# Attention of the second and third token tile eight heads at a time, first loads in a fixed order, and two other matmul orders in layer 2

## The chip, the core and the metric

The kernel runs on one core of one Trainium2 chip. The time is device microseconds of one execution. A core has five instruction streams that run beside each other and wait for one another by semaphores: TensorE (PE, matmuls; its weight loads are shown as PEld), VectorE (DVE), ScalarE (ACT), GpSimd (POOL) and SyncE (SP, which here issues every DMA). Each stream is executed in the order in which it is written.

## What is computed

A local and global attention over 2 batches, 8 heads, 768 positions and 64 columns a head, followed by two feed-forward layers over the 1536 tokens. Cut to what matters:

```python
# attention: a window of +-15 positions, and 24 block summaries (blocks of 32)
k_sum = k.reshape(B, H, nb, block, D).max(axis=3)
v_sum = v.reshape(B, H, nb, block, D).mean(axis=3)
scores_l = scale * q @ k^T, -1e9 outside |i - j| < 16
scores_s = scale * q @ k_sum^T + log(32)
a = softmax(concatenate([scores_l, scores_s]))
attn = a @ concatenate([v, v_sum])
# two layers, 512 -> 2048 -> 512 each
h = x @ w_in;  g = h * sigmoid(1.702 * h);  x = g @ w_out      # layer 1
h = x @ w_in;  g = h * cos(h);              x = g @ w_out      # layer 2
```

All is float32. The feed-forward products are made of three matmuls each, on a high and a low part of both operands (high x high, low x high, high x low).

## The kernel before

**Tiles.** Tokens go in three tiles of 512 (`U`). A layer works through the 16 slices of 128 of `d_ff`, tile after tile: 48 steps a layer, 96 in all. A step has 12 matmuls of 512 columns for `h` (`ff_h`, lines 651 to 653: four slices `k` of the input by three products) and 12 for the output (`ff_out`, lines 744 to 746: four slices `d`, each into its own bank `acc0` to `acc3`). So there are 2304 of these matmuls, here called the FF matmuls. Between `h` and `out` stands the gate (`ff_gate`, ScalarE and VectorE). The weights come packed from memory, one `raw` tile of 1024 KB for two slices (`w_load`), and `convert` takes them apart into high and low part on ScalarE and VectorE: `w scale`, `w low`, `w join`, two `w hi`, two `w lo`. In layer 1 this runs about a step ahead of its use.

**Attention.** A unit (`att`) is 128 queries of four heads: scores `s` (TensorE, line 425), mask and maximum `ttr` (VectorE, line 434, one instruction a head), `exp` (ScalarE, line 443), the sum and its reciprocal (lines 450, 452) and `norm` (line 456) on VectorE, the transposes `t` (TensorE, line 461), their copy `at` (ScalarE, line 465), and the products with the values `pv` (TensorE, line 472). For the first token tile (`early`, eight units) `xc` (ScalarE, line 504) and `xl` (VectorE, line 507) then write the input `xh` of layer 1. The first `h` matmul of slices k = 0, 1 needs the four units of heads 0 to 3, that of k = 2, 3 the other four. The 16 units of the second and third tile (`main_unit`) are spread over the steps 0 to 30, between FF matmuls; their `xc` (line 519) writes `xf`.

**Loads.** All of `k` (`kf`) and 512 queries (`qf`) of the first batch are loaded for the early units. The values come as windows of 96 rows, four heads at a time (`load_v`, line 314), into `win` and `vy`; the main units have windows of `k` and `q` too (`load_k`, line 325, and `load_q`). The block means of `v` are made from `vf`: sums on POOL (line 371), a matmul `vs_ps` (line 382) and copies into the last 24 rows of each window (`put_vsum`, lines 349 and 353). Those of the second batch take seven sums on POOL and one matmul, `vsum1`.

**What sets the order.** Every step is an `Op` with a kind, an engine, a cost and what it depends on. `order_of` lists them by urgency, the length of the chain behind an `Op` plus a number for its kind from the table `BONUS`, and the program is written out in that order, for all engines and for the DMA issues of SP. The `Ring`s are the buffers: PSUM banks `a0`, `a1`, `acc0` to `acc3` and two `h`, the slots of the weights, `raw`, `win` and others.

## Time and profile before

| | |
|---|---|
| median of 3 runs | 607.96 us (607.31 to 608.61) |
| profiled execution, own time | 610.31 us |
| its span, first to last instruction | 608.5 us |
| TensorE busy in the span | 589.0 us |
| VectorE, ScalarE, GpSimd busy | 402.7, 298.4, 17.0 us |
| first FF matmul starts | 43.93 us |
| last FF matmul starts | 604.53 us |

A matmul's record is longer than the distance to the next one, because matmuls are pipelined; whether TensorE is held up is read from the distances of the starts. Records on VectorE and ScalarE overlap a little in the same way. A waiting time is put down to the engine whose semaphore came last.

### The profile page before, as it was taken

The numbers are of one execution on the slowest core, as the hardware profiler recorded it, in microseconds if no ns is written. First come the engines' busy times: TensorE is split into PE (matmuls) and PEld (weight loads), VectorE is DVE, ScalarE is ACT, GpSimd is POOL, SyncE is SP. The second block draws the span as 40 slices with busy tenths as digits, with TensorE's granted clock in tenths as the row PEclk, the third lists the DMA queues.
The fourth block names the chain that finished last, engine by engine and source line by source line (L and its number), as shares of the span: only waits on it lengthen the run. The fifth ranks groups of instructions, "written<-read, shape, count | busy, mean of one in ns | idle before, by whom it ended". The sixth has DMA issues, their size and how long they took to land.

```text
span 608.5 us, 8715 instructions
## 1 busy us (share of the span) xinstructions
PE 589.0 (97%) x3310; PEld 474.1 (78%) x3310; DVE 402.7 (66%) x826; ACT 298.4 (49%) x617; POOL 17.0 (3%) x20
## 2 busy tenths in 40 slices
PE   7759999999999999999999999999999999999997
PEld 4547777777777888888888888888888888888886
DVE  5688999965444432467778876667756668666664
ACT  4677788755544322356556643234433334433332
POOL 3240000000000000000000000000000000000000
PEclk8879999999999999999999999999999999999999
DMA  8998778552120500025553000000100000100001
GB/s 293 227 279 280 254 253 270 193 181 71 56 49 23 208 1 1 0 71 205 178 181 128 1 2 0 1 0 1 57 13 0 1 2 0 70 1 1 0 1 69
DMA packets 27817, 55.07 MB, mean 91 GB/s; under 512 B 10752, under 2 KB 19840, under 8 KB 23680
## 3 DMA queue, kind: packets, MB, share of 16 engines
q1 hardware_dynamic: 27776, 54.52, 27.3%
q8 instruction: 26, 0.43, 0.3%
q14 instruction: 15, 0.12, 0.1%
HBM read 51.37 MB, written 3.15 MB: 90 GB/s over the span
## 4 chain that ended last, share of the span: by engine, by line
PE 91%; DMA 4%; DVE 2%; ACT 1%; issue 1%; SPq 0%; ACTq 0%
PE h_ps L651 15%; PE acc L744 15%; PE h_ps L652 14%; PE h_ps L653 14%; PE acc L745 14%; PE acc L746 14%; PE x_ps L472 2%; PE t_ps L461 2%; PE s_ps L425 2%; DMA kf<-in_kT_dram 1%; DMA vf<-in_v_dram 1%; DMA raw<-in_w_dram 1%; DVE ex L434 0%; DVE ex L456 0%; DVE z L450 0%
## 5 line engine op out<-in xcount | busy, mean ns | idle before, releaser
L651 PE MATMUL h_ps<-xh,w 128*128 128x512 f32 x384 | 153.2, 399 | 0.0
L744 PE MATMUL acc<-g,w 128*128 128x512 f32 x384 | 151.4, 394 | 0.0
L652 PE MATMUL h_ps<-xh,w 128*128 128x512 f32 x384 | 150.1, 391 | 0.0
L653 PE MATMUL h_ps<-xh,w 128*128 128x512 f32 x384 | 150.1, 391 | 0.0
L745 PE MATMUL acc<-g,w 128*128 128x512 f32 x384 | 149.6, 390 | 0.0
L746 PE MATMUL acc<-g,w 128*128 128x512 f32 x384 | 149.6, 390 | 0.0
L705 ACT CAST g<-gt 128x512 fp32r<-128x512 f32 x96 | 59.7, 622 | 125.1 <-PE acc L746 121.7
L709 DVE TENSOR_TENSOR g<-gt,g 128x512 fp32r<-128x512 f32 x96 | 66.1, 689 | 65.9 <-ACT g L705 65.9
L744 PEld LDWEIGHTS acc<-g,w 128*128 128x128 f32 x384 | 72.1, 188 | 16.6 <-issue 1.7
L651 PEld LDWEIGHTS h_ps<-xh,w 128*128 128x128 f32 x384 | 72.3, 188 | 15.8 <-issue 0.6
L653 PEld LDWEIGHTS h_ps<-xh,w 128*128 128x128 f32 x384 | 72.4, 189 | 15.4
L746 PEld LDWEIGHTS acc<-g,w 128*128 128x128 f32 x384 | 72.1, 188 | 15.2
L745 PEld LDWEIGHTS acc<-g,w 128*128 128x128 f32 x384 | 72.1, 188 | 14.4
L652 PEld LDWEIGHTS h_ps<-xh,w 128*128 128x128 f32 x384 | 72.5, 189 | 14.0
L697 ACT ACTIVATE gt<-gt,half_pi 128x512 f32<-128x512 f32 x48 | 34.7, 723 | 62.1 <-DVE gt L693 62.1
L673 ACT ACTIVATE gt<-h_ps 128x512 f32<-128x512 f32 x48 | 28.7, 598 | 54.1 <-PE h_ps L653 53.8
L681 DVE TENSOR_SCALAR gt<-gt 128x512 f32<-128x512 f32 x48 | 20.5, 427 | 48.3 <-ACT gt L673 47.9
L701 DVE TENSOR_TENSOR gt<-gt,h_ps 128x512 f32<-128x512 f32 x48 | 33.0, 687 | 26.2 <-ACT gt L697 26.2
L603 DVE TENSOR_TENSOR w<-wc,w 128x512 fp32r<-128x512 f32 x64 | 42.9, 686 | 0.3 <-ACT w L599 0.3
L582 DVE SCALAR_TENSOR_TENSOR wc<-wc,raw 128x1024 uint32<-128x1024 uint32 x32 | 39.3, 1229 | 2.4 <-ACT wc L572 1.4
L572 ACT ACTIVATE wc<-raw 128x1024 f32<-128x1024 f32 x32 | 37.1, 1160 | 6.0 <-DMA raw<-in_w_dram 5.5
L599 ACT CAST w<-wc 128x512 fp32r<-128x512 f32 x64 | 38.4, 621 | 0.4 <-DVE wc L582 0.3
(66 smaller groups left out, 494.8 us busy)
## 6 DMA issues: line engine op xcount, KB each, us to landing
raw<-in_w_dram SPq DMA_DIRECT2D x32, 1024.0 KB, 5.0
win<-in_v_dram SPq DMA_DIRECT2D x40, 96.0 KB, 3.0
win<-in_kT_dram SPq DMA_DIRECT2D x32, 96.0 KB, 3.3
out_dram<-xf SPq DMA_DIRECT2D x12, 256.0 KB, 2.0
win<-in_qT_dram SPq DMA_DIRECT2D x16, 128.0 KB, 3.2
kf<-in_kT_dram SPq DMA_DIRECT2D x4, 400.0 KB, 6.1
k<-in_kT_dram SPq DMA_DIRECT2D x4, 400.0 KB, 5.6
vf<-in_v_dram SPq DMA_DIRECT2D x3, 512.0 KB, 7.4
```

What stands on the lines that cost most here:

```text
L572: nc.scalar.activation(out=t.bitcast(FP32), in_=raws[m][:, :, 1].bitcast(FP32), func=ACTF.Prelu, scale=REBIAS, alpha=SIGN)
L582: nc.vector.scalar_tensor_tensor(out=t, in0=t, scalar=3, in1=raws[m][:, :, 0], op0=ALU.logical_shift_left, op1=ALU.bitwise_or)
L599: nc.scalar.copy(out=w[:, 0, :], in_=mids[m][:, 512 * a:512 * (a + 1)].bitcast(FP32))
L603: nc.vector.tensor_tensor(out=w[:, 1, :], in0=mids[m][:, 512 * a:512 * (a + 1)].bitcast(FP32), in1=w[:, 0, :].bitcast(FP32), op=ALU.subtract,)
L651: nc.tensor.matmul(out=hs[i], lhsT=w[:, 0, c], rhs=x[:, 0, :], start=(k == 0), stop=False)
L652: nc.tensor.matmul(out=hs[i], lhsT=w[:, 1, c], rhs=x[:, 0, :], start=False, stop=False)
L653: nc.tensor.matmul(out=hs[i], lhsT=w[:, 0, c], rhs=x[:, 1, :], start=False, stop=(k == KD - 1))
L705: nc.scalar.copy(out=g[:, 0, :], in_=gts[i])
L709: nc.vector.tensor_tensor(out=g[:, 1, :], in0=gts[i], in1=g[:, 0, :].bitcast(FP32), op=ALU.subtract)
L744: nc.tensor.matmul(out=o, lhsT=w[:, 0, c], rhs=g[:, 0, :], start=(f == 0), stop=False)
L745: nc.tensor.matmul(out=o, lhsT=w[:, 1, c], rhs=g[:, 0, :], start=False, stop=False)
L746: nc.tensor.matmul(out=o, lhsT=w[:, 0, c], rhs=g[:, 1, :], start=False, stop=(f == NF - 1))
```

## The change

**Units.** The early part keeps its eight units of four heads (`early_unit`). The second and third tile get eight units of all eight heads (`main_unit`): 16 instead of 8 score matmuls in a row, eight `ttr` and eight `exp`, one sum and reciprocal, two `norm`, eight transposes, two `at`, 16 instead of 8 products, one `xc`. Numbers (`nm`, `z`, `r`) lie beside the scores and no longer in a pool of their own; the main units' buffers `sm_main` and `at_main` are slots of `w1`, those of the early units six and four deep instead of three.

**Loads.** Windows of `v` are laid out by the host (`vwin`) and come for all heads in one DMA with 4 KB a row. The list `wanted` makes each of the first loads wait for the issue of the one before it, and what comes later waits for the last of them.

**Layer 2.** In `ff_h` the products of low weights come first, so that the second and third matmul of a slice have the same weights. In `ff_out` two slices `d` go side by side: each product for `d` and `d + 1` in turn, into two banks.

**The table.** `BONUS` has other numbers, and some costs are other ones.

```diff
 BONUS = {
-    "at": 1927.8, "early at": -1746.5, "early exp": 2659.8, "early load w": -427.0, "early norm": -4559.3,
+    "at": 6913.9, "early at": 11300.1, "early exp": -9024.5, "early load v": -3298.6, "early load w": -5638.8,
...
-PUT_VSUM = ("ACT", "POOL")
+PUT_VSUM = ("ACT", "POOL", "POOL")
...
-    at_early = [ex[0][:, 512 * j:512 * j + 512] for j in range(3)]
-    sm_early = [ex[0][:, 1536:2016], ex[1][:, 0:480], ex[1][:, 480:960]]
+    sm_early = [ex[j // 4][:, 512 * (j % 4):512 * (j % 4) + 512] for j in range(6)]
...
-        def fn():
-            for g in range(2):
-                nc.sync.dma_start(out=dst[0:GW, g, :], in_=v[b, 128 * j + 64 * g:128 * j + 64 * g + GW, c])
-
-        return op("load v", "DMA", 0.8, fn, *deps)
+        return dma(("early " if i < UT else "") + "load v", 1.5, dst[0:GW].rearrange("p g d -> p (g d)"), vwin[i], *deps)
...
+    def main_unit(i, kq_deps, v_deps, space, rings, extra):
+        st, heads = {}, range(H)
...
+        def s_fn():
+            st["s"] = [bank(t, "s_ps")[:, 0:4 * GC].rearrange("p (h c) -> p h c", h=4) for t in ("a0", "a1")]
+            scores(s_ps, heads, [(slice(0, GC), lambda hp, g: (qw[:, hp, :], kw[:, hp, g, :]))])
...
+        def pv_fn():
+            st["x"] = bank("a0", "x_ps").rearrange("p (h q) -> p h q", h=4)
+            values(lambda h: st["x"][:, h // 2, :], heads, at, vw)
...
-                nc.tensor.matmul(out=hs[i], lhsT=w[:, 0, c], rhs=x[:, 0, :], start=(k == 0), stop=False)
-                nc.tensor.matmul(out=hs[i], lhsT=w[:, 1, c], rhs=x[:, 0, :], start=False, stop=False)
-                nc.tensor.matmul(out=hs[i], lhsT=w[:, 0, c], rhs=x[:, 1, :], start=False, stop=(k == KD - 1))
+                passes = ((0, 0), (1, 0), (0, 1)) if layer == 0 else ((1, 0), (0, 0), (0, 1))
+                for n, (a, b) in enumerate(passes):
+                    nc.tensor.matmul(
+                        out=hs[i], lhsT=w[:, a, c], rhs=x[:, b, :], start=(k == 0 and n == 0),
+                        stop=(k == KD - 1 and n == 2),
+                    )
...
+        beside = 1 if layer == 0 else 2
+        for d0 in range(0, KD, beside):
+            def fn(d0=d0):
+                w, g = wt[layer, 1, f], gs[i]
+                for n, (a, b) in enumerate(((0, 0), (1, 0), (0, 1))):
+                    for d in range(d0, d0 + beside):
...
+    wanted = [d_kf[0], d_kf[1], d_qf[0], d_mask, d_kf[2], d_kf[3], d_qf[1], d_id, d_blk, *d_vf[0], d_v[0], w_loads[0],
+              *d_v[1:], w_loads[1]]
+    for x, y in zip(wanted, wanted[1:]):
+        y.deps.append((x,))
...
-    due = dict(zip((*range(0, 16, 2), *range(16, 32, 2)), range(U0, NU)))
+    due = dict(zip((0, 3, 7, 10, 16, 20, 24, 28), range(UT, NU)))
```

Three places show how the instructions move. The first is SP's queue at the start. Before, `vf` is the values for the block means, `kf` and `qf` keys and queries, `win` and `vy` windows, `raw` weights:

```order
L253 DMA kf<-in_kT_dram 128x800 x2
L253 DMA qf<-in_qT_dram 128x2x512
L253 DMA mask_sb<-in_maskc_dram 128x360
L253 DMA vf<-in_v_dram 128x1024
L253 DMA ident<-in_identc_dram 128x128
L253 DMA vf<-in_v_dram 128x1024
L253 DMA ex<-in_blkc_dram 128x256
L253 DMA vf<-in_v_dram 128x1024
L314 DMA win<-in_v_dram 96x256 x2
L253 DMA kf<-in_kT_dram 128x800 x2
L253 DMA qf<-in_qT_dram 128x2x512
L314 DMA vy<-in_v_dram 96x256 x4
```

and with the change, from the third row of the same queue on:

```order
L252 DMA mask_sb<-in_maskc_dram 128x360
L252 DMA kf<-in_kT_dram 128x800 x2
L252 DMA qf<-in_qT_dram 128x2x512
L252 DMA ident<-in_identc_dram 128x128
L252 DMA ex<-in_blkc_dram 128x256
L252 DMA vf<-in_v_dram 128x1024 x3
L252 DMA win<-in_vwin_dram 96x1024
L592 DMA raw<-in_w_dram 128x2048
L252 DMA vy<-in_vwin_dram 96x1024 x3
L592 DMA raw<-in_w_dram 128x2048
L252 DMA win<-in_qT_dram 128x4x128
L316 DMA win<-in_kT_dram 128x4x96 x2
```

The second half of the keys and queries now stands ahead of `vf`, and both first weight loads ahead of all windows of the main units and of the second batch; before, the first weight load stood behind 34 other DMAs, five of them windows of keys and queries for main units and three of them `vf` of the second batch.

The second place is TensorE's queue where the early part ends. Before (`x_ps` from `ex` is an early `pv`, the last `x_ps` row here that of the first main unit):

```order
L472 MATMUL x_ps<-ex,vy 64x64 x8
L651 MATMUL h_ps<-xh,w 128x512
L652 MATMUL h_ps<-xh,w 128x512
L653 MATMUL h_ps<-xh,w 128x512
L651 MATMUL h_ps<-xh,w 128x512
L652 MATMUL h_ps<-xh,w 128x512
L653 MATMUL h_ps<-xh,w 128x512
L472 MATMUL x_ps<-ex,win 64x64 x8
L461 MATMUL t_ps<-ident,ex 120x128 x4
L472 MATMUL x_ps<-ex,win 64x64 x8
```

and with the change (`at_early` is an early `pv`, `sm_main` and `at_main` the first main unit of eight heads, `vs_ps` the block means of the second batch):

```order
L685 MATMUL h_ps<-xh,w 128x512 x3
L431 MATMUL x_ps<-at_early,vy 64x64 x8
L685 MATMUL h_ps<-xh,w 128x512 x3
L451 MATMUL t_ps<-ident,ex 120x128 x4
L509 MATMUL t_ps<-ident,sm_main 120x128 x4
L431 MATMUL x_ps<-at_early,vy 64x64 x8
L509 MATMUL t_ps<-ident,sm_main 120x128 x4
L431 MATMUL x_ps<-at_early,vy 64x64 x8
L431 MATMUL x_ps<-at_main,win 64x64 x16
L365 MATMUL vs_ps<-vf,ex 120x512
L685 MATMUL h_ps<-xh,w 128x512 x15
L402 MATMUL s_ps<-win 64x120 x16
```

In both, six FF matmuls stand ahead of the last early units and all others behind them. With the change a whole main unit and `vs_ps` stand ahead of the seventh FF matmul too; before, `vs_ps` stood behind 48 of them.

The third place is the output of a step of layer 2 on TensorE (`acc2` and `acc3` are the banks, the instructions of one slice of `d_ff`). Before:

```order
L744 MATMUL acc2_4547<-g_4827,w_3037 128x512
L745 MATMUL acc2_4547<-g_4827,w_3037 128x512
L746 MATMUL acc2_4547<-g_4827,w_3037 128x512
L744 MATMUL acc3_4555<-g_4827,w_3037 128x512
L745 MATMUL acc3_4555<-g_4827,w_3037 128x512
L746 MATMUL acc3_4555<-g_4827,w_3037 128x512
```

and with the change:

```order
L780 MATMUL acc2_4364<-g_4502,w_2683 128x512
L780 MATMUL acc3_4366<-g_4502,w_2683 128x512
L780 MATMUL acc2_4364<-g_4502,w_2683 128x512
L780 MATMUL acc3_4366<-g_4502,w_2683 128x512
L780 MATMUL acc2_4364<-g_4502,w_2683 128x512
L780 MATMUL acc3_4366<-g_4502,w_2683 128x512
```

The bank changes with each matmul and no longer with each third.

## Rows read from the trace of the kernel before

**Rows 1.** Stages: us, busy PE, PEld, DVE, ACT, POOL; granted clock, DMA share, GB/s.

```profile
0.00:8.70 8.70, 5.85 (x48) 2.65 (x52) 2.00 (x5) 1.49 (x2) 0.99 (x6) 1.00 0.75 244
8.70:49.70 41.00, 28.28 (x433) 21.21 (x425) 31.69 (x118) 27.28 (x98) 15.16 (x12) 0.75 0.92 267
49.70:110.00 60.30, 59.96 (x410) 46.02 (x408) 57.45 (x132) 50.37 (x115) 0.86 (x2) 1.00 0.80 271
200.01:604.75 404.74, 404.74 (x1788) 335.08 (x1785) 261.21 (x426) 170.41 (x270) 0.00 (x0) 1.00 0.12 43
```

**Rows 2.** TensorE in order of time, its end: start us, us, instruction.

```profile
600.45 0.39 PE L746 MATMUL acc<-g,w 128*128 128x512 f32 x1
...
604.53 0.39 PE L746 MATMUL acc<-g,w 128*128 128x512 f32 x1
```

**Rows 3.** TensorE in order of time, one main unit between FF matmuls.

```profile
182.95 0.64 PE L425 MATMUL s_ps<-win 64*64 64x120 f32 x16
183.52 0.50 PE L744 MATMUL acc<-g,w 128*128 128x512 f32 x1
...
188.46 0.60 PE L461 MATMUL t_ps<-ident,room 128*120 128x128 f32 x4
188.81 0.48 PE L651 MATMUL h_ps<-xh,w 128*128 128x512 f32 x1
...
190.38 0.73 PE L472 MATMUL x_ps<-room,win 120*64 120x64 f32 x16
191.04 0.50 PE L651 MATMUL h_ps<-xh,w 128*128 128x512 f32 x1
...
191.94 0.64 PE L425 MATMUL s_ps<-win 64*64 64x120 f32 x16
```

**Rows 4.** TensorE in order of time, first FF matmuls and start of their stream.

```profile
44.52 0.63 PE L652 MATMUL h_ps<-xh,w 128*128 128x512 f32 x1
44.95 0.63 PE L653 MATMUL h_ps<-xh,w 128*128 128x512 f32 x1
...
49.70 0.50 PE L651 MATMUL h_ps<-xh,w 128*128 128x512 f32 x1
```

**Rows 5.** VectorE's waits, 8.70 to 49.70 us: us in total, times, longest.

```profile
DVE xh L507 <- ACT xh L504: 2.3, 2, 1.4
DVE ex L363 <- DMA kf<-in_kT_dram: 1.6, 2, 1.0
DVE raw L578 <- DMA raw<-in_w_dram: 1.4, 1, 1.4
DVE ex L363 <- DMA k<-in_kT_dram: 1.0, 1, 1.0
```

**Rows 6.** VectorE's groups, 8.70 to 49.70 us: count | busy us, mean ns.

```profile
L456 DVE TENSOR_TENSOR ex<-ex,r 128x480 f32<-128x480 f32 x9 | 8.4, 931 | 0.1
L434 DVE CUSTOM_DVE_ANT_0 ex<-s_ps,mask_sb 128x120 f32<-128x120 f32 x36 | 7.9, 276 | 3.3 <-PE s_ps L425 3.3
...
L582 DVE SCALAR_TENSOR_TENSOR wc<-wc,raw 128x1024 uint32<-128x1024 uint32 x2 | 2.6, 1299 | 0.0
...
L603 DVE TENSOR_TENSOR w<-wc,w 128x512 fp32r<-128x512 f32 x3 | 2.0, 683 | 0.3 <-ACT w L599 0.3
```

**Rows 7.** GpSimd and VectorE in order of time, both at work in SBUF.

```profile
27.78 1.27 POOL L371 TENSOR_TENSOR vf<-vf 96x512 f32<-96x512 f32 x1
...
28.11 1.46 DVE L456 TENSOR_TENSOR ex<-ex,r 128x480 f32<-128x480 f32 x1
```

**Rows 8.** Block means of the second batch: GpSimd's last sums, TensorE's matmul.

```profile
37.92 4.82 POOL L371 TENSOR_TENSOR vf<-vf 96x512 f32<-96x512 f32 x3 [3.53 <-DMA vf<-in_v_dram]
...
60.68 1.02 PE L382 MATMUL vs_ps<-vf,ex 96*120 96x512 f32 x2
61.63 0.73 PE L472 MATMUL x_ps<-ex,win 120*64 120x64 f32 x16
```

More of the change, by code (lines that the diff above doesn't have):

```diff
@@ new lines @@
+    "at": 6913.9, "early at": 11300.1, "early exp": -9024.5, "early load v": -3298.6, "early load w": -5638.8,
+    "early norm": 1236.7, "early pv": -17013.0, "early s": 2629.4, "early sum": -13980.0, "early t": 19910.9,
+    "early ttr": -9137.8, "early w hi": -13120.7, "early w join": 7985.0, "early w lo": -5404.2,
+    "early w low": 3146.8, "early w scale": -7999.3, "early xc": 347.7, "early xl": -392.8, "evac": 996.7,
+    "exp": 3462.7, "g hi": -5363.1, "g lo": -20315.4, "gate": 13512.3, "h": 1261.1, "ksum": -10120.9,
@@ new lines, in edge, with scores @@
+    def edge(i):
+        return {0: 0, NTILE - 1: 2}.get(i % NTILE, 1)
+    def scores(ps, heads, parts):
+        for c, part in parts:
+            for h in heads:
+                p0 = 64 * (h % 2)
+                for g in range(2):
+                    q, k = part(h // 2, g)
+                    nc.tensor.matmul(
+                        out=ps(h)[64 * g:64 * g + 64, c], lhsT=q[p0:p0 + 64, 64 * g:64 * g + 64],
+                        rhs=k[p0:p0 + 64], start=True, stop=True,
+                    )
@@ new lines, in normed, with values @@
+    def normed(sm, r):
+        n = sm.shape[1]
+        r = r.rearrange("p (h o) -> p h o", o=1)
+        nc.vector.tensor_tensor(out=sm, in0=sm, in1=r.to_broadcast([128, n, GC]), op=ALU.mult)
+    def values(ps, heads, at, vv):
+        for h in heads:
+            p0 = 64 * (h % 2)
+            for g in range(2):
+                nc.tensor.matmul(
+                    out=ps(h)[p0:p0 + 64, 64 * g:64 * g + 64], lhsT=vv[:, g, D * h:D * (h + 1)],
+                    rhs=at(h)[:, 64 * g:64 * g + 64], start=True, stop=True,
+                )
@@ L478, in att @@
         for t in s_tags:
             ring[t].take(s)
-        ttr = op(stage + "ttr", "DVE", 0.84, ttr_fn, s, d_mask)
-        for t in s_tags:
             ring[t].use(ttr)
-        ex_ = op(stage + "exp", "ACT", 1.52, exp_fn, ttr)
-        sm_o = op(stage + "sum", "DVE", 0.3, sum_fn, ex_)
-        nrm = op(stage + "norm", "DVE", 0.57, norm_fn, sm_o)
-        tt = op(stage + "t", "PE", 0.44, t_fn, nrm, d_id)
-        ring[t_tag].take(tt)
+        ring["acc2"].take(tt)
+        ring["acc2"].use(ac)
@@ L488, in att @@
+        ring["acc3"].take(pv)
+        ring["acc3"].use(xc)
+        ring["acc3"].use(xl)
         sm_ring.take(ttr)
[L489 removed]
+        for x in (e, zr, nrm, tt):
             sm_ring.use(x)
[L491 to L492 removed]
         at_ring.take(ac)
[L494 removed]
         at_ring.use(pv)
[L496 to L498 removed]
@@ L751, in ff_out @@
             ring["g"].use_of(g_last[i][1], o)
-            if f == 0:
-                ring[f"acc{d}"].take(o)
-            else:
-                ring[f"acc{d}"].use(o)
-            res.append(o)
+            for d in range(d0, d0 + beside):
+                if f == 0:
+                    ring[f"acc{d}"].take(o)
+                else:
+                    ring[f"acc{d}"].use(o)
+                res.append(o)
         if f == NF - 1:
@@ L893, in main_unit @@
[L893 to L904 removed]
+        if i + 1 == NU:
+            return
```

498 lines of the change are left out of this document (233 added, 265 removed).

## The prediction, made blind

> **What bounds the kernel now.** I read the trace in three steps. First the busy times by stage [rows 1] and TensorE's starts at the end [rows 2]: from 600.45 to 604.53 us lie 18 distances of 0.2267 us, and from 200 us to the end TensorE has no gap at all. The granted clock is full there, 2.4 GHz, at which 512 columns are 0.2133 us. So the 2304 FF matmuls cost 522.3 us, and nothing in the change takes one of them away. Second, TensorE with attention between the FF matmuls [rows 3]: it still never waits, it only has more to do. From 182.95 to 191.94 us, 8.99 us, stand 30 FF matmuls (6.80 us) and one main unit, so a unit costs TensorE 2.19 us. Of this `s` is 0.57, `t` 0.35 and `pv` 0.66 us, together 1.58; the other 0.61 goes at the three changes of work. Third, the start of the stream [rows 4]: six FF matmuls come early, the seventh starts at 49.70 us, and from there on TensorE is held up nowhere by more than some tenths. So the time is three terms: when the stream of FF matmuls starts, what stands in it beside 2298 x 0.2267 = 520.9 us, and the tail of 3.75 us behind the last matmul at 604.53 us. The other engines matter before 49.70 us alone. VectorE, at 57.45 of 60.30 us, is nearly full until 110 us [rows 1], but TensorE did not wait for it.
>
> **The start of the stream.** Before 49.70 us TensorE is not the bound. Every early unit passes through VectorE four times, and VectorE is busy for 2.00 + 31.69 = 33.7 us of it [rows 1]. It is idle for 6.7 us before 8.70, when the first keys, queries and the mask come, and for 9.3 us after. The first four DMAs are the same ones with the change, so the 6.7 us stay. Of the 9.3 us, 4.0 are waits for keys of either batch and for the first weights (1.6 + 1.4 + 1.0), and 2.3 are one for ScalarE [rows 5], whose own queue stood behind the same weight load: its `w scale` is ahead of an `at` that the next `pv` needs. The fixed order of loads takes these away: keys and queries come next after the mask, `raw` ahead of all windows of main units. I count 6.3 us gone and 3.0 left. Next late after these waits is VectorE itself.
>
> What VectorE must do before the stream grows. Counted in the two orders, it has four more `ttr` (4 x 0.28), a `norm` (0.93), a `w join` (1.30) and a `w lo` (0.68) ahead of the last early `xl` [rows 6]: 4.0 us. Its work and the first idle time give a floor of 33.7 + 6.7 + 4.0 = 44.4 us. With 3.0 us of other waits the stream starts at 47.4 us, with all 9.3 us of before at 53.7. The waits left are those of one `pv` for the `xl` of the last (one bank, `acc3`) and of `t` for `at` (`acc2`), which the change keeps. They are shorter than all of before and not nothing, so I take 47.4, which is 2.3 us earlier than before. A price in both is GpSimd's: a `norm` that met a GpSimd sum took 1.46 us, 0.52 of it after GpSimd was done [rows 7]. GpSimd has twelve such operations with the change and eleven before, which is within the bounds.
>
> New in front of the stream are a whole main unit and `vs_ps`, and on SP the window of values for that unit: it waits for the fifth early `pv`, and behind it on SP stands the third weight load, whose `w scale` is ahead of the last early `xc` on ScalarE. If that load is late, the stream is. It has some 6 us between that `pv` and its use, by the spacing of 2.7 us that I give the units, so I cost it at nothing.
>
> **In the stream.** Before, TensorE's time from 49.70 to 604.76 us is 555.1, so 34.2 us are not FF matmuls. `vs_ps` is 0.95 of it [rows 8]; the other 33.25 are 15 units and the `t` and `pv` of the first, some 15.7 units, or 2.12 each. A unit of eight heads has twice the matmuls and the same three changes of work: 2 x 2.12 - (2.12 - 1.58) = 3.70 us. Seven of them stand in the stream, 25.9 us. That is 8.3 us less: 4.7 because a unit and `vs_ps` now run where TensorE waits anyway, and 3.6 for the changes of work. The cost of a change has no row of its own with the new sizes. It lies between 0 and twice that, so the 3.6 between 0 and 7; I take it, since both sides of each change are the same instructions.
>
> Against this I set three small costs. The stream may begin at half clock: the first FF matmuls ran 0.43 us apart [rows 4], six of them, 1.2 us lost, where the clock of the stage was 0.75 on the mean [rows 1]. At the new start TensorE does as little ahead; 1.0, between 0 and 2.4. The last main unit has only nine FF matmuls (2.0 us) between its `pv` and the third tile's first `h`, with `xc`, `x hi` and `x lo` in between, and eight `exp` in a row make each chain longer: 0.5, between 0 and 2. The last two output slices now end together and their stores come at once: 0.2, between 0 and the 0.7 of three matmuls. VectorE's later load is not larger: what it does for the step of the stream is the same, and one main unit is already done.
>
> **The orders of layer 2.** Before, each matmul is 0.2267 us after the last, whether the bank or the weights or the moving side changed: along the 18 distances [rows 2] all three kinds of change occur. Every matmul still has its own weight load with the change. So I cost both orders at nothing. A gain is possible where two matmuls in a row have the same weights, 192 times in layer 2, by at most the 0.0133 us above 512 columns: 2.6 us. A loss is possible too, by the same 2.6, since nothing shows banks in turn at every matmul.
>
> [...]
>
> **The sum.** Start -2.3, stream -8.3, half clock +1.0, held up +0.5, tail +0.2: -8.9 us. On the profiled execution's own 610.31 us this is 601.4. That execution was 2.35 us above the median of the three runs, 607.96, and I forecast against the median: **599.1 us**.
>
> **The rivals.**
> - VectorE without idle time after 8.70 us: start at 44.4, 596.1 us. For it: its queue is dense in the new order. Against it: one bank each for `t` and `pv`, so units follow each other through three engines.
> - VectorE keeps all its idle time, the loads having only hidden other waits: start at 53.7, 605.4 us. For it: 3 us of a main unit's `exp` now stand ahead of an early `xc` on ScalarE.
> - Slower than before: `vs_ps` holds the stream. It stood behind 48 FF matmuls; now it is directly ahead of the seventh, and seven GpSimd sums lead to it. Ahead of the last of its loads are 10.95 MB, by the sizes of the DMAs. At 267 GB/s [rows 1] these end at 41.0 us; three sums in 4.82 us and 0.95 us of matmul follow [rows 8], 46.8 us, just at my start. The gain is used up when the start is at 56.3, so at 217 GB/s or below; at 200 GB/s the start is 60.5 and the time 612.2 us. For it: no slack. Against it: the slowest stage had 244, and rows of 4 KB replace those of 1 KB.
> - A weight that stays costs less: 2.6 us less, 596.5 us. Against it: no weight load is left out.
> - Banks in turn bring layer 2 to the bare 512 columns: 1152 x 0.0133 = 15.3 us less, 583.8 us. Against it: outputs change bank at each third distance before, and the distance is the same. [...]
>
> **How the numbers follow.** My forecast, a start between 45 and 52 us, has 0.60; VectorE without idle 0.14; with all of it 0.14; `vs_ps` 0.06; the weight that stays 0.04; banks in turn 0.02. The range of 594.0 to 605.0 leaves out the last of these, `vs_ps` and about half of the case with all idle time, with some of the forecast's outer parts: under 0.2. What a measurement can tell from no change is about 0.2%, 1.2 us. Faster by more than that (below 606.7) hold the forecast, the cases without idle and with layer 2, and most of the case with all idle time: 0.91. Within it lies the rest of that case and a little of `vs_ps`, 0.04; slower 0.05.
>
> **What would show it.** The seventh FF matmul starts near 47 us, ahead of it stands an `xl` or `vs_ps`, and VectorE's idle time after 8.7 us is near 3 us: the first term. From there to the end TensorE has no gaps, seven units with `s` near 1.15 and `pv` near 1.3 us, and 25.9 us beside FF matmuls: the second. A distance in layer 2 other than 0.2267 us would overturn the fourth part, a start behind 56 us the sign, and gaps of TensorE between 50 and 110 us would mean that VectorE or ScalarE had become the bound of the first tile.

## The result and the profile after

| | before | with the change |
|---|---|---|
| median (lowest to highest) | 608.29 us (606.89 to 608.99) | 602.53 us (601.49 to 604.91) |
| profiled execution, own time | 610.31 us | 603.28 us |
| its span | 608.5 us | 601.5 us |
| first FF matmul | 43.93 us | 38.08 us |
| start of the stream (seventh FF matmul) | 49.70 us | 51.39 us |
| stream, from there to the last FF matmul's start | 554.83 us | 545.49 us |
| from there to the end of the span | 4.00 us | 4.62 us |

The ratio of the changed kernel to the one before is 0.9913, with an interval of 0.9889 to 0.9937: faster by 5.8 us. Forecast were 599.1 us, 8.9 less, and a range of 594.0 to 605.0. The sign is right and the time lies in the range, but a third of the gain is missing. In the two profiles the difference is 7.0 us, and the three terms give it: the start +1.69, the stream -9.34, the tail +0.62.

**The stages.** The columns are those of [rows 1]: us, busy PE, PEld, DVE, ACT, POOL, granted clock, DMA share, GB/s.

```profile
0.00:8.70 8.70, 6.26 (x70) 3.09 (x70) 2.44 (x9) 1.60 (x3) 0.99 (x6) 1.00 0.78 269
8.70:49.70 41.00, 33.01 (x440) 24.29 (x435) 33.59 (x125) 29.80 (x106) 17.33 (x13) 0.68 1.00 289
25.00:48.00 23.00, 17.10 (x175) 13.14 (x177) 16.93 (x40) 14.89 (x52) 10.17 (x7) 0.68 1.03 287
51.39:110.00 58.61, 58.61 (x290) 48.17 (x289) 56.10 (x95) 43.44 (x80) 2.66 (x2) 1.00 0.71 254
200.00:596.90 396.90, 396.90 (x1953) 327.82 (x1951) 270.17 (x498) 184.01 (x337) 0.00 (x0) 1.00 0.15 51
```

From 8.70 to 49.70 us the DMA share is 1.00, before 0.92, and the granted clock of TensorE is lower, 0.68 after 0.75. Behind 51.39 us TensorE is busy all the time, as before. VectorE, at 56.10 of 58.61 us, is as full as it was.

**The stream.** TensorE in order of time, one unit of eight heads between FF matmuls, answering to [rows 3]:

```profile
198.39 1.05 PE L402 MATMUL s_ps<-win 64*64 64x120 f32 x32
199.37 0.98 PE L685 MATMUL h_ps<-xh,w 128*128 128x512 f32 x3
...
205.67 1.03 PE L509 MATMUL t_ps<-ident,room 128*120 128x128 f32 x8
206.46 0.94 PE L780 MATMUL acc<-g,w 128*128 128x512 f32 x3
...
208.71 1.20 PE L431 MATMUL x_ps<-room,win 120*64 120x64 f32 x32
209.84 0.98 PE L685 MATMUL h_ps<-xh,w 128*128 128x512 f32 x3
...
211.44 1.05 PE L402 MATMUL s_ps<-win 64*64 64x120 f32 x32
```

From one unit's scores to the next, 13.05 us, stand 42 FF matmuls (9.52 us) and one unit: 3.53 us. Scores are 0.98, transposes 0.79, products 1.13 us by the distances of the starts, together 2.90; the three changes of work take 0.63, as much as the 0.61 of a unit with half the heads.

**The end.** TensorE's last 15 matmuls, and VectorE's last copy:

```profile
593.71 3.56 PE L780 MATMUL acc<-g,w 128*128 128x512 f32 x15
...
597.31 0.69 DVE L805 COPY xf<-acc 128x512 f32<-128x512 f32 x1 [0.67 <-PE acc L780]
```

15 matmuls from the first's start to the last's end are 3.56 us: 14 distances of 0.2267 and one record of 0.39, with two banks in turn as with one [rows 2].

**The start.** The chain that ended last, cut at 60 us, in order of time (start us, us, what):

```profile
19.84 14.53 DMA win<-in_kT_dram
...
34.41 1.87 PE s_ps L402 x30
...
36.31 1.71 DVE sm_main L409 x16
38.02 0.34 DVE xh L469
38.36 2.79 DVE w L635 x2
41.15 0.86 DVE ex L346
...
42.58 1.45 DVE sm_main L425
...
44.07 1.11 PE t_ps L509 x4
45.18 1.11 PE x_ps L431 x16
46.29 1.04 PE t_ps L509 x4
47.33 2.81 PE x_ps L431 x48
50.14 0.72 issue
50.86 1.09 PE vs_ps L365 x2
```

The first main unit of eight heads is this chain. Its scores wait for the window of keys, which lands at 34.4 us at the end of a full DMA queue. VectorE stands ahead of its masks for 1.9 us, with work of early units and weights queued behind. Then come its masks, an `xl`, two `w lo` (2.79 us), a block maximum, and its `sum` and `norm`. The last two early `pv` stand behind its `t` on TensorE, at half clock (a `t` of four is 1.11 us here, 0.65 at full clock). `vs_ps` waits 0.72 us more, until the copy of the main unit's `x_ps` on ScalarE (50.18 to 50.76 us) has freed the bank `a0`. VectorE's waits from 8.70 us to the last early `xl` (us in total, times, longest):

```profile
DVE sm_main L409 <- PE s_ps L402: 1.9, 1, 1.9
DVE wc L614 <- ACT wc L604: 1.8, 2, 1.3
DVE ex L419 <- ACT ex L416: 1.8, 2, 1.0
DVE xh L469 <- ACT xh L468: 1.1, 1, 1.1
DVE raw L610 <- DMA raw<-in_w_dram: 0.2, 1, 0.2
```

The waits of [rows 5] for keys and weights are down from 4.0 to 0.2 us, as the fixed order of loads should do. But 6.6 us of others have come, where 3.0 were forecast.

### The profile page after: what moved, and what is told of

It is laid out like the page before. It is cut to its first block, busy times and chain, and to the rows that moved or that the text cites. A ratio compares the mean times of both kernels' runs of the same rounds, so it can differ in the third digit from the quotient of the medians.

```text
span 601.5 us, 8594 instructions
## 1 busy us (share of the span) xinstructions
PE 586.1 (97%) x3310; PEld 477.5 (79%) x3310; DVE 400.8 (67%) x810; ACT 295.7 (49%) x607; POOL 21.0 (3%) x21
## 4 chain that ended last, share of the span: by engine, by line
PE 92%; DMA 5%; DVE 1%; SPq 0%; issue 0%
PE acc L780 44%; PE h_ps L685 43%; DMA win<-in_kT_dram 2%; PE x_ps L431 2%; DMA win<-in_vwin_dram 2%; PE s_ps L402 1%; PE t_ps L509 1%; DMA kf<-in_kT_dram 1%; DVE w L635 0%; DVE sm_main L409 0%; SPq L252 0%; DVE sm_main L425 0%; PE vs_ps L365 0%; DVE ex L346 0%; DVE xf L805 0%
## 5 line engine op out<-in xcount | busy, mean ns | idle before, releaser
L685 PE MATMUL h_ps<-xh,w 128*128 128x512 f32 x1152 | 300.6, 392 | 0.0
L780 PE MATMUL acc<-g,w 128*128 128x512 f32 x1152 | 299.9, 391 | 0.0
L712 DVE SCALAR_TENSOR_TENSOR gt<-gt,h_ps 128x512 f32<-128x512 f32 x48 | 32.8, 684 | 26.6 <-ACT gt L706 26.6
L708 ACT ACTIVATE gt<-h_ps 128x512 f32<-128x512 f32 x48 | 28.7, 597 | 38.1 <-PE h_ps L685 38.1
L604 ACT ACTIVATE wc<-raw 128x1024 f32<-128x1024 f32 x32 | 36.6, 1142 | 10.2 <-DVE w L635 7.0
L706 ACT ACTIVATE gt<-h_ps 128x512 f32<-128x512 f32 x48 | 28.4, 592 | 26.4 <-PE h_ps L685 26.2
L716 DVE TENSOR_SCALAR gt<-gt 128x512 f32<-128x512 f32 x48 | 20.5, 426 | 31.0 <-ACT gt L708 30.9
L720 DVE SCALAR_TENSOR_TENSOR r<-gt,h_ps 128x512 f32<-128x512 f32 x48 | 33.4, 697 | 1.7
L724 DVE SCALAR_TENSOR_TENSOR gt<-gt,r 128x512 f32<-128x512 f32 x48 | 32.9, 686 | 1.4
L610 DVE TENSOR_SCALAR raw<-raw 128x1024 uint32<-128x1024 uint32 x32 | 22.3, 697 | 4.3 <-DMA raw<-in_w_dram 4.3
L728 DVE TENSOR_SCALAR gt<-gt 128x512 f32<-128x512 f32 x48 | 20.4, 424 | 0.9
L660 DVE TENSOR_TENSOR xh<-xf,xh 128x512 fp32r<-128x512 f32 x20 | 13.1, 687 | 4.7 <-ACT xh L657 3.9
L416 ACT ACTIVATE ex<-ex 128x120 f32<-128x120 f32 x32 | 12.2, 383 | 6.4 <-DVE ex L409 6.4
```

The lines of the kernel that those rows point to most:

```text
L604: nc.scalar.activation(out=t.bitcast(FP32), in_=raws[m][:, :, 1].bitcast(FP32), func=ACTF.Prelu, scale=REBIAS, alpha=SIGN)
L685: nc.tensor.matmul(out=hs[i], lhsT=w[:, a, c], rhs=x[:, b, :], start=(k == 0 and n == 0), stop=(k == KD - 1 and n == 2),)
L720: nc.vector.scalar_tensor_tensor(out=r, in0=gts[i], scalar=-C1, in1=hs[i], op0=ALU.mult, op1=ALU.add)
L724: nc.vector.scalar_tensor_tensor(out=gt, in0=gt, scalar=-C2, in1=rs[0], op0=ALU.mult, op1=ALU.add)
L780: nc.tensor.matmul(out=accs[d][:, 0:U], lhsT=w[:, a, 128 * d:128 * (d + 1)], rhs=g[:, b, :], start=(f == 0 and n == 0), stop=(f == NF - 1 ...
```

## Experiments

Theories on the missing part, which all lie ahead of 51.39 us. W: the window of keys lands late, since the DMA queue is the bound. G: GpSimd's seven sums stretch VectorE. M: the main unit's transposes hold the early `pv` on TensorE. Later X (weight conversions stand ahead of what the start needs), D (W, and the third weight load as a second place) and C (TensorE's half clock). All kernels are the changed one with one edit or, where it is said, several. In those that move work the list of `Op`s is sorted as in the changed kernel, some get another place, and what depends on them follows. Masks is the start of the first main unit's masks; masks, start and stream are from each kernel's profile, which is one execution. The kernel before was timed anew beside each set of runs, with medians from 608.29 to 609.94 us, so differences of 1 to 2 us between two kernels' medians say little by themselves; the intervals of the ratios say more.

| kernel | median (range), us | ratio to before [interval] | masks | start | stream |
|---|---|---|---|---|---|
| changed | 602.53 (601.49 to 604.91) | 0.9913 [0.9889, 0.9937] | 36.31 | 51.39 | 545.49 |
| e8_again | 602.78 (600.52 to 603.27) | 0.9890 [0.9872, 0.9908] | 36.62 | 50.90 | 545.49 |
| e1_orders | 600.73 (599.83 to 601.98) | 0.9860 [0.9834, 0.9886] | 34.59 | 48.30 | 545.49 |
| e2_nosums | 602.35 (601.79 to 604.47) | 0.9894 [0.9861, 0.9926] | 38.66 | 50.42 | 545.50 |
| e3_halfvf | 601.28 (601.15 to 601.98) | 0.9870 [0.9848, 0.9892] | 34.19 | 49.42 | 545.48 |
| e9_cover | 596.76 (595.01 to 600.33) | 0.9788 [0.9765, 0.9811] | 37.58 | 48.42 | 545.48 |
| e10_fill | 601.30 (600.26 to 602.01) | 0.9863 [0.9838, 0.9887] | 34.76 | 48.46 | 547.09 |
| e4_behind | 608.23 (606.79 to 610.70) | 0.9979 [0.9962, 0.9996] | 38.53 | 48.11 | 553.83 |
| e5_window | 604.59 (600.77 to 606.25) | 0.9923 [0.9895, 0.9951] | 33.94 | 48.87 | 545.50 |
| e6_conv | 605.12 (602.72 to 607.84) | 0.9936 [0.9910, 0.9961] | 38.82 | 52.66 | 548.79 |
| e7_both | 604.55 (603.16 to 606.09) | 0.9925 [0.9905, 0.9945] | 35.28 | 49.02 | 550.15 |
| e11_ahead | 606.71 (602.32 to 607.91) | 0.9947 [0.9926, 0.9968] | 39.00 | 50.20 | 550.92 |
| e12_aheadfill | 605.37 (601.06 to 607.78) | 0.9929 [0.9904, 0.9955] | 35.82 | 49.26 | 550.97 |

**The two orders of layer 2 undone.**

```diff
-                passes = ((0, 0), (1, 0), (0, 1)) if layer == 0 else ((1, 0), (0, 0), (0, 1))
+                passes = ((0, 0), (1, 0), (0, 1))
...
-                for n, (a, b) in enumerate(((0, 0), (1, 0), (0, 1))):
-                    for d in range(d0, d0 + beside):
+                for d in range(d0, d0 + beside):
+                    for n, (a, b) in enumerate(((0, 0), (1, 0), (0, 1))):
```

> The changed kernel with both matmul orders of layer 2 as they were before; the order of every engine's other work is the same. Theory: both orders cost and give nothing between the matmuls, so the FF matmuls of layer 2 stay 0.2267 us apart and the stream (51.39 to 596.88 us, 545.5 us) keeps its length within 0.3 us. Only the end changes: from the last FF matmul to the end of the span it took 4.6 us with the new order and 4.0 in the kernel before, so the tail should be about 0.6 us shorter, span 600.9. Rival, that the new orders gain something by weights that stay: distances of 0.229 or more in layer 2 and a span over 603.

The stream is 545.49 us with either order: the orders are worth nothing between matmuls. The tail is 4.26 instead of 4.62 us, 0.36 shorter. What was not expected is the start, 48.30 us, 3.1 earlier with the same program up to there. TensorE in order of time there:

```profile
32.65 1.35 PE L402 MATMUL s_ps<-win 64*64 64x120 f32 x32
...
47.77 1.09 PE L365 MATMUL vs_ps<-vf,ex 96*120 96x512 f32 x2 [0.72 <-issue]
48.30 3.98 PE L685 MATMUL h_ps<-xh,w 128*128 128x512 f32 x15
```

and its stage from 25 to 48 us:

```profile
25.00:48.00 23.00, 15.98 (x211) 12.53 (x212) 18.81 (x46) 16.04 (x50) 9.72 (x7) 0.85 1.05 280
```

In this execution the window of keys landed at 32.9 us, when the scores had just come up (32.65), and the granted clock was 0.85. So one program starts its stream at different times: the six executions of the changed kernel had spans of 599.7 to 603.1 us, which makes starts of 49.6 to 53.0 if all have 545.49 and 4.62 us behind them. The median of this variant is 1.8 us below the changed kernel's, 0.36 of it by the tail; whether the rest is more than scatter of the start is not settled.

**The changed kernel again.** No edit.

> The changed kernel itself again, beside the three variants of this call. From its first matmul of the stream to its last it took 545.49 us in the first profile and in two variants that leave this part alone, to 0.01 us, so what differs between executions is the start of the stream, 49.6 to 53.0 us by the spans of its six runs. Expected: stream 545.49 us again, start anywhere in 48 to 53, time 600.5 to 604, median near 602. If the stream itself varies, the reading that all scatter lies ahead of it falls.

The stream again has 545.49 us, and the start, 50.90, lies in the span named. From here on a profile's start is compared together with its masks and its clock.

**Without the seven sums on GpSimd.**

```diff
-            done.append(vsum_add(1, "POOL", t[:, 0, :], t[:, 1, :], d_vf[1][a]))
+            done.append(ring["w1"].use_of(3 + a, op("vsum1 add", "POOL", 1.22, lambda: None, d_vf[1][a])))
...
-            done[x] = vsum_add(1, "POOL", vf[1][x][:, 0, :], vf[1][y][:, 0, :], done[x], done[y])
+            done[x] = op("vsum1 add", "POOL", 1.22, lambda: None, done[x], done[y])
```

> The changed kernel without the seven GpSimd sums for the block means of the second batch (they are left out, so that the block means are those of a part of the rows). Theory G: these sums, at work from 36.10 to 46.78 us, stretch what VectorE does beside them (two w lo 2.87 us where one is 0.69 alone, two norm 1.44 and 1.38 where one is 0.65), 3.0 us in all, and the chain to the stream's start goes through these: start near 48.4 instead of 51.39, span near 598.5. Theories W (the first main unit's window of keys lands late) and M (that unit's transposes stand ahead of the last early pv on TensorE): VectorE then waits elsewhere, start at 50.9 or later, span 601 or more.

The median moved by 0.2 us: G alone does not set the start, which at 50.42 us is 2.0 later than G expected and 0.5 earlier than W and M did. Yet what G names is there. From masks to start it is 11.8 us instead of 15.1. In this profile the gain goes to DMAs: the window landed later still (36.7 us), and then the third weight load became the last (chain of waits):

```profile
20.72 16.00 DMA win<-in_kT_dram
...
40.19 7.58 DMA raw<-in_w_dram
...
47.87 1.19 ACT wc L604
49.06 0.26 ACT xh L468
```

`w scale` (L604) waits for the weight load, and the `xc` that the last `xl` needs stands behind it on ScalarE.

**Half the bytes of the first three `vf` loads.**

```diff
-            d_vf[b].append(ring["w1"].take(dma(("load vf", "load vf1")[b], (1.46, 1.5)[b], t, r[a]), True))
+            d_vf[b].append(ring["w1"].take(dma(..., t if b else t[:, 0, :], r[a] if b else r[a][:, 0, :]), True))
...
-            o = vsum_add(0, "POOL", t[:, 0, :], t[:, 1, :], d_vf[0][a])
+            o = vsum_add(0, "POOL", t[:, 0, :], t[:, 0, :], d_vf[0][a])
```

> The changed kernel with half the bytes of the three vf loads of the first batch (only one of the two rows of each partition is loaded and added to itself): 0.79 MB less ahead of all windows and weights, everything else the same. Theory W: the DMA queue is the bound up to 34.4 us (8.97 MB at about 276 GB/s), so the window of keys of the first main unit lands 2.8 us earlier, near 31.6, VectorE's wait of 1.9 us ahead of that unit's masks goes, and the stream starts up to 2.8 us earlier, 48.6; span near 598.7. Theories G and M: the window lands earlier, but the start moves by under 1 us.

Some 1.3 us faster than the changed kernel by the medians, half of what W would give; the interval of the ratio overlaps with both of the changed kernel's. The window landed at 32.1 us, the scores came up at 32.28 and did not wait, the masks at 34.19 without VectorE's wait of 1.9; from there to the start it is 15.2 us as before. That fits W for the first half of the chain, and no further. It does not show it: e1_orders, with all the bytes, had its window at 32.9 us and its masks at 34.59.

**Both, with half of all seven `vf` loads.** The edit of the sums above, and every `vf` load with half its rows: the three of e3_halfvf and the four of the second batch, which stand between the window of keys and the third weight load.

> The changed kernel with half the bytes of all seven vf loads (both batches, 1.57 MB less) and without the seven GpSimd sums of the second batch; block means are wrong in both. Alone, half of the first three loads brought 1.3 us by the medians, and leaving out the sums nothing. Theory D (the DMA queue holds the start at two places, the window of keys ahead of the first main unit and then the third weight load, and GpSimd's sums hide behind it): window 2.8 us and weight load 5.6 us earlier, VectorE not stretched by 3 us: masks of the main unit near 34.2, from there 12 us to the start, 46.3; time near 597.7. Theory C (TensorE at half clock makes each early unit longer, whatever the loads do): start 48.5 or later, time 600 or more.

5.8 to 6.0 us faster than the changed kernel, the one gain that is clear of all scatter, where the sums alone had brought 0.2 and three loads 1.3. So loads and sums together hold more of the start than the 3.1 us that are missing. It fits D: they stand beside each other on the way to the start, and each one covers what the other one gives back. But half of the four other loads was not tried alone, and by D it takes away just the wait that e2_nosums ran into; how much of the 6 us is theirs is not shown. The profile here is the slowest of its executions, and its window still came late (landed at 35.6 us, masks 37.58), so D's earlier masks (34.2) are not seen in it. From there it was 10.8 us to the start, and the third weight load, 5.4 us from issue to landing, was not waited for. One stage shows that the queue is no longer full:

```profile
35.00:40.00 5.00, 4.87 (x54) 4.08 (x55) 3.29 (x20) 2.29 (x8) 0.00 (x0) 0.50 0.17 42
```

**Fillers on TensorE where it waits.**

```diff
+        early = sorted((o for o in ops if o.kind == "early pv"), key=ops.index)
+        fill = {early[1]: 3, early[2]: 3, early[3]: 3, kinds(ops, "s")[0]: 3, kinds(ops, "t")[0]: 4}
         for o in order_of(ops):
+            if o in fill:
+                to = bank("a1", "fill") if o.kind == "t" else wps
+                for _ in range(fill[o]):
+                    nc.tensor.matmul(out=to[:, 0:128], lhsT=ident, rhs=ident, start=True, stop=True)
             o.fn()
```

> The changed kernel with 16 matmuls more on TensorE (128 columns in float32, into a bank that nothing reads), at places where it waited for other engines: three ahead of each of three early pv, three ahead of the first main unit's scores, four ahead of its first t. They change no result. Theory C: the granted clock between 25 and 48 us rises from 0.66 (0.5 to 1.0 by stages) towards 1.0, each t and pv of 1.1 to 1.2 us takes 0.65 to 0.73, ten of them and the main pv give 3 to 4 us, the start comes at 48.0 or earlier: time 600 or below. Theory D: the clock may rise, but the window of keys and the third weight load come when they come; start within 0.7 us of 51, time 602 to 603.5, or up to 1 us later by the fillers' own time.

The stage from 25 to 48 us (columns as above):

```profile
25.00:48.00 23.00, 16.06 (x237) 13.14 (x237) 17.91 (x43) 17.07 (x55) 9.76 (x7) 1.00 1.06 285
```

and TensorE in order of time, the start of the stream:

```profile
47.93 1.09 PE L365 MATMUL vs_ps<-vf,ex 96*120 96x512 f32 x2 [1.82 <-issue]
48.46 5.59 PE L685 MATMUL h_ps<-xh,w 128*128 128x512 f32 x15
```

The clock stays at its full level and the start comes at 48.46 us, 2.4 to 2.9 earlier than in the changed kernel's two profiles, but no earlier than in e1_orders (48.30), which has no fillers and the same program up to there. Ahead of the start TensorE waits 1.82 us ahead of `vs_ps` (the third weight load landed at 45.9, with `w scale`, the last `xc` and the copy that frees `a0` behind it), falls to half clock, and the first 15 FF matmuls take 1.6 us more than in the changed kernel. By the medians 1.2 to 1.5 us are left. C may be a part of the cause: from masks to start it was 13.7 us here and in e1_orders, with clocks of 1.00 and 0.85, 14.3 in e8_again with 0.80, and 15.1 and 15.2 in the changed kernel and e3_halfvf with 0.68 and 0.70. The interval of the ratio overlaps with one of the changed kernel's two and lies just below the other, and that of e1_orders does the same without fillers. So a gain by the fillers is not shown.

**The main unit's second half behind the start.** Six `Op`s of the unit and `vs_ps` get places behind the last `xl` and among the first 36 FF matmuls. The next unit's scores move with them, from 21 FF matmuls in to 42; its transposes stay behind 57.

```diff
+    for kind, n, at in (("sum", 1, xl), ("norm", 2, xl), ("t", 2, h[6]), ("pv", 1, h[9])):
+        for k, o in enumerate(kinds(ops, kind)[:n]):
+            key[o] = at + 0.1 + 0.1 * k
+    key[kinds(ops, "vsum1")[0]] = h[11] + 0.1
+    key[kinds(ops, "s")[1]] = h[13] + 0.1
```

> The changed kernel with the second half of the first main unit of eight heads (sum, both norm, t, at, pv, xc) and vs_ps moved behind the stream's start, between the first 36 FF matmuls; scores, masks and exp stay where they are. Theory M: the last two early pv stand behind t of the main unit, which waits for norm 2.1 us; without it the start is near 47.0, and the stream gets 0.79 + 1.13 + 0.44 us and some 0.6 for changes of work, 3.0 us: span near 600.1, faster by 1.4. If W or G alone set the start, it stays at 50 or later and the span is 603 or more.

The start is 48.11 us although the window landed 2.2 us later than in the changed kernel, 9.6 us behind the masks, where the changed kernel's two profiles have 15.1 and 14.3 and e1_orders 13.7. So M holds for the start. But the stream is 8.3 us longer, not 3.0. TensorE in order of time:

```profile
49.84 5.32 PE L685 MATMUL h_ps<-xh,w 128*128 128x512 f32 x13 [0.52 <-DVE xh L469]
...
69.49 1.19 PE L509 MATMUL t_ps<-ident,sm_main 128*120 128x128 f32 x8 [1.79 <-DVE sm_main L425]
```

The first FF matmuls run at half clock (eleven distances of 0.43 to 0.59 us), after TensorE had waited 1.4 us ahead of them and 0.5 between them, and 20 us later the next unit's `norm` is late on VectorE. That last wait, 1.8 us, comes with the later scores and so with this edit's places; other places were not tried. Ahead of the stream the unit is done where both engines would wait anyway, and it keeps TensorE at work.

**The window of keys ahead of the second weight load.**

```diff
+    for k, o in enumerate((kinds(ops, "load q")[0], kinds(ops, "load k")[0])):
+        o.deps = [d for d in o.deps if d != (load[1],)]
+        key[o] = key[load[1]] - 0.3 + 0.1 * k
+    put("early w low", 1, sorted(xl)[4] + 0.1)
+    put("early w scale", 1, max(key[o] for o in kinds(ops, "exp")[:2]) + 0.1)
+    put("early w join", 1, max(key[o] for o in kinds(ops, "norm")[:2]) + 0.1)
+    put("early w hi", 2, max(xl) + 0.01), put("early w lo", 2, max(xl) + 0.02)
```

> The windows of keys and queries of the first main unit are loaded ahead of the second weight load instead of behind it; the conversion of that weight load (w low, w scale, w join, one w hi, one w lo) moves behind the main unit's masks and exp, so that nothing stands in VectorE's queue for it. Theory W (the window of keys, which lands at the end of a DMA queue that is never idle, holds the first main unit's masks and with them the start): 1.05 MB less ahead of it are 3.7 us at 280 GB/s; masks begin 2 to 3.7 us earlier than 36.3, the start comes about 2 us earlier, 600.5 or below. Theory X (weight conversions on VectorE and ScalarE ahead of what the start needs): no gain over 0.5 us, since the same conversions still stand ahead of the last xl.

In the profiled execution, 600.77 us, it did what W says: masks at 33.94, start at 48.87. But it is the fastest; the others took 604.57 to 606.25 us, slower than the changed kernel, and the median misses W's 600.5. What they lose is not shown by this profile, and stays open.

**Conversions of weights behind the last `xl`.** `early w hi` and `early w lo` number 2, a block maximum, and `w scale`, `w low`, `w join` of the third load, each `key` set just behind the last `early xl`.

> Loads as in the changed kernel; the conversion of the third weight load (w scale, w low, w join), one w hi and w lo of the second and the first block maximum of the second batch's keys move behind the last early xl. Theory X: ahead of the main unit's sum VectorE then has nothing (it began 1.1 us after the last exp), and the last xl no longer stands behind a w join that waits for w scale (it came 1.9 us after its xc could be done): start 1.5 us earlier, about 601.0. Theory W: the window of keys still sets when the main unit begins, but what follows is shorter all the same, so W expects less than X, 0.5 us. Neither expects gaps in the stream; if the conversions come too late there, h of slice 2 waits some 5 us behind the start and the gain is lost.

Slower by 2.3 to 2.6 us by the medians. TensorE waits in the stream 1.7 us for the copy of `vs_ps`, which now stands behind `w scale` on ScalarE, and 1.3 us for a gate that VectorE did late. From masks to start it is 13.8 us, within the 13.7 to 15.1 of the changed kernel's profiles and e1_orders, so X's 1.5 us are not shown there, and what was put off comes back in the stream.

**Both of the last two, `vs_ps` behind six FF matmuls.**

> Both of the last two, and vs_ps six FF matmuls behind the start of the stream instead of directly ahead of it. W and X together: masks 2 to 3.7 us earlier, and 1.5 us less from there to the last xl; vs_ps costs 0.45 to 0.55 us in the stream in place of 0.6 ahead of it. Start near 47.5, time near 599.0, faster than the changed kernel by 3. If only one of them holds, 600.5; if the DMA queue or GpSimd's sums bind behind them, 601 to 602.

Slower by 1.8 to 2.0 us by the medians, where a gain of 3 was expected. Start 49.02, stream 4.7 us longer, and a DMA again: the main unit's products waited 2.1 us for its window of values, landed at 47 us.

**The third weight load's conversion alone behind the start,** with the old orders of layer 2, and `vs_ps` and one block maximum moved too; once without fillers, once with (three ahead of each place of e10_fill, two more ahead of the seventh FF matmul).

```diff
+    key[min(kinds(ops, "ksum")[4:], key=key.get)] = xl[6] + 0.05
+    key[kinds(ops, "early w lo")[3]] = xl[7] + 0.02
+    for k, kind in enumerate(("vsum1", "vsb", "w scale", "w low", "w join")):
+        key[kinds(ops, kind)[0]] = h[3] + 0.1 + 0.02 * k
+    gate = kinds(ops, "gate")
+    for k in range(2):
+        key[kinds(ops, "w hi")[k]] = key[gate[0]] + 0.01 + 0.01 * k
+        key[kinds(ops, "w lo")[k]] = key[gate[1]] + 0.01 + 0.01 * k
```

> The changed kernel with the old orders of layer 2 (tail 0.35 us shorter), and what stood ahead of the start without need moved: the third weight load's w scale, w low and w join behind the last early xc and xl and behind vs_ps, vs_ps six FF matmuls into the stream, one block maximum of keys from ahead of the main unit's sum to VectorE's wait after it. No loads are moved. Theory D: the wait for the third weight load (1.5 us in two profiles) no longer stands ahead of the last xc; 0.9 us less ahead of the main unit's t; start some 2 us earlier than the 51 of the changed kernel, vs_ps 0.5 us in the stream: time near 600.5. Theory C: TensorE waits as much as before and may enter the stream at half clock, with 1 to 2 us lost there: 601 to 602.5.

> The last one with fillers on TensorE (three ahead of each of three early pv, of the first main unit's scores and its first t, two ahead of the seventh FF matmul). If C and D both hold and add up: granted clock near 1.0 from 25 us on, start near 46.5, stream 546 us with vs_ps in it, time near 597.5, faster than the changed kernel by 5 us. If the fillers gain only because they cover the same waits as the moved conversions, it is no faster than the kernel without them, within 1 us.

Both are slower than the changed kernel, by 2.6 to 4.2 us and so by more than either theory expected, at starts that are 0.7 to 2.1 us earlier than its two profiles' (from masks to start 11.2 and 13.4 us). The waits of TensorE from 45 to 110 us (us in total, times, longest) in the first of them, of which those for `sm_main` lie ahead of the start and the one for `gt` in the stream:

```profile
PE h_ps L685 <- DVE gt L712: 3.0, 1, 3.0
PE t_ps L509 <- DVE sm_main L425: 2.0, 2, 1.7
```

A step's gate on VectorE (L712) is late, since the conversions, a unit's masks and the gates now come together there. TensorE waits, the FF matmuls behind come 0.43 us apart for a while, and both kernels' streams have 5.4 to 5.5 us more. The fillers brought neither the start of 46.5 nor the gain that was hoped for: the two kernels' intervals overlap, and the clock from 25 to 48 us was 0.87 with them and 0.70 without.

## Why the prediction held, and where it failed

**The number and the mechanism.** The time lies in the range, and the start in the outer part of the forecast's 45 to 52 us, but two misses partly cancel: the start came 4.0 us later than its sum, and the stream, forecast 6.8 us shorter with both costs set against it, came 9.3 shorter. That they cancel is luck.

**What bounds the kernel**: right. In seven profiles of kernels that leave the stream alone it is 545.48 to 545.50 us; the time of an execution is its start and this.

**The start of the stream**: the step that failed. Forecast was 47.4 us, 2.3 earlier than before; it came at 51.39, and 50.90 the second time. The two sums made there stand differently. VectorE's work was well counted: 33.7 + 4.0 = 37.7 us forecast, and 2.44 us to 8.70 and 34.05 from there to 50.16 us measured, 36.5. The first idle time was 6.3 us, not 6.7. The term that was mis-sized is "6.3 us gone and 3.0 left": VectorE was idle for 7.4 of the 41.46 us, 4.4 more than the 3.0, and 6.8 of the 7.4 are the waits shown above. The prediction had named an idle time near 3 us as a sign that its first term holds. With 1.2 us less work, 0.4 less at first, 4.4 more of waits and 1.2 from the last `xl` over `vs_ps` to the stream, the miss is 4.0. The old waits did go. (The 2.3 us for ScalarE that the prediction calls one wait were two, of up to 1.4; its sum is the same.) I looked for the next late one in VectorE's own work, and named the banks, but not the window of keys of the unit that the change puts in front: it lands at 34.4 us as the last of 9.0 MB, and in the nine profiles with the same loads ahead of it it landed between 32.9 and 37.1 us. The other 4.7 us are waits for ScalarE's `w scale`, `exp` and `xc`, which in turn stood behind TensorE's `t` and `pv` at half clock and behind one another. That loads and sums hold the start together is what e9_cover shows; that each covers the other, and that the clock is a third cause, fits e2_nosums, e3_halfvf and the clocks named under e10_fill, but no run separates them.

**GpSimd's price** was called within the bounds. It is larger than I took it for, in one place, some 3.0 us: its sums (now 9.13 us in a row from 37.65 us on) meet two `w lo` and the main unit's `norm`.

```profile
38.27 2.87 DVE L635 TENSOR_TENSOR w<-wc,w 128x512 fp32r<-128x512 f32 x2
41.07 0.94 DVE L346 TENSOR_REDUCE ex<-k 128x24 f32<-128x768 f32 x1
...
42.58 1.44 DVE L425 TENSOR_TENSOR sm_main<-sm_main 128x480 f32<-128x480 f32 x1
43.94 0.41 DVE L469 TENSOR_TENSOR xh<-x_ps,xh 128x256 fp32r<-128x256 f32 x1
```

A `w lo` is 0.69 and a `norm` 0.65 us where GpSimd rests; the block maximum (0.94) and `xl` (0.41) are not longer. The Trainium skill, on its page "SBUF — State Buffer" under "Who interferes with whom", says that a VectorE instruction with two inputs in SBUF contends with a GpSimd instruction that reads there, and one with at most a single such input doesn't, outside the modes that use both ports; by that rule `w lo` and `norm` suffer and the other two don't, and the trace agrees, as does e2_nosums: without the sums a `norm` of the main unit is 0.65 and 0.66 us there.

**The third weight load** was costed at nothing, with 6 us of cover. The cover was used up: the load took 7.6 us from issue to landing in the profile of the changed kernel, 9.7 in e8_again and 10.1 in e1_orders. VectorE did not wait for it in the first of these, but 1.4 us in e1_orders, and in e8_again, the same kernel, as here:

```profile
DVE raw L610 <- DMA raw<-in_w_dram: 1.3, 1, 1.3
```

In e2_nosums it ended the chain. So costing it at nothing did not hold in every execution.

**`vs_ps`**: the rival named the right resource, the DMA queue, and the wrong transfer. Its sums were to end near 45.8 us and it near 46.8; the sums ended at 46.78 (37.65 + 9.13). What it waited for then was the bank, not the loads.

**The stream**: 9.34 us less. Forecast were 8.3 less for units and `vs_ps`, with 1.0 for half clock and 0.5 for units that hold it up against it. Beside 2297 distances of 0.2267 us are 24.8 us, 0.4 at the first distance (0.63 us) and the rest for seven units, 3.5 each, where 3.70 were forecast: the price of twice the matmuls was a little lower (2.90 for 3.16), that of a change of work the same, as assumed. Half clock cost nothing, where 1.0 was forecast: the granted clock is 1.00 from the start on, and the first distance is as long (0.64) in e11_ahead, where `vs_ps` stands among FF matmuls 0.23 us apart, so it belongs to the place behind `vs_ps`. TensorE had waited 0.72 us ahead of it. With 1.8 us of wait at the same place e10_fill lost 1.6 us by half clock, and e4_behind 2.5, without the unit and `vs_ps` ahead. The last unit's nine FF matmuls were enough, nothing waited there.

**The orders of layer 2**: nothing, as costed; the rivals of a weight that stays and of banks in turn fall with e1_orders, whose stream is as long. The tail was 0.62 us longer for a forecast 0.2, inside its bound of 0.7; 0.36 of it came with the new orders, by e1_orders.

**What stays open**: the share of each load, of the sums and of the clock in the late start. The fixed order of loads by itself was not tried; the waits that it took away and those that came are only seen in the traces. Why e5_window's other executions were slow is not known. No version with right results was found that clearly beats the changed kernel: e10_fill and e1_orders lie 1.2 to 2.1 us below it, about the scatter of its start.

## What to carry to other kernels

When a change puts a whole unit of work in front of the point that everything waits for, follow that unit's own loads to their landing as carefully as the waits that go: here the window was the last of 9.0 MB in a full queue, and its landing moved by 4 us from one execution to another besides. Where several causes may run side by side to one point, taking one away can measure little; take them away together, and then each part of the edit alone, before one is named. Compare a variant's profile with several profiles of the same program, since a start that is 3 us earlier came without any edit ahead of it. And work moved behind the start is not free: with VectorE 95% full there, as here, it came back as waits of TensorE in the stream in all five variants that did it, in e11_ahead and e12_aheadfill for a gate of VectorE and with half clock on top.

## What the runs showed of the hardware beyond that

The same loads in the same order had landed between 32.9 and 37.1 us in different executions, while 545 us of matmuls behind them repeat to 0.02 us. The granted clock of the same program between 25 and 48 us was 0.68, 0.80 and 0.85; with 16 small matmuls at places of waiting it was 1.00 in the one profile (e10_fill), with 17 and another order of work 0.87 (e12_aheadfill). In e4_behind, e7_both, e10_fill, e11_ahead and e12_aheadfill FF matmuls came 0.43 us apart after TensorE had waited 1.4 to 3.0 us; in e6_conv, after waits of 1.7 and 1.3 us, and in e2_nosums, after 1.6, they did not.
